# A recurrence and a gated feed-forward in one kernel: all steps put in a new order by a new table of due times

## The chip, the cores and the metric

The kernel runs on one core of a Trainium2 chip. The metric is the device time of one execution in microseconds (us). Before the change it is 270.87 us, the median of 13 runs that lie between 267.84 and 272.73 us.

## What is computed

The reference first runs a gated recurrence over 768 tokens for 4 batches and 8 heads of 48 columns each, and then a feed-forward layer with a sigmoid gate on its output:

```python
new_re = ar * S_re - ai * S_im
new_im = ar * S_im + ai * S_re
S_re, S_im = (new_re + kv, new_im)
y[:, :, t] = np.einsum('bhd,bhde->bhe', q[:, :, t], S_re)
...
gate = 1.0 / (1.0 + np.exp(-(x @ w_gate)))
val = x @ w_val
return (gate * val @ w_out).astype(np.float32)
```

Here `kv` is the outer product of a token's k and v, `ar` and `ai` are a decay of limited size, and x is y with the heads put side by side (3072 tokens of 384). The weights are 384 x 1536 (gate, value) and 1536 x 384 (out).

## The kernel before

**Tiles.** The work is cut into 24 slabs of 128 tokens: slab m is chunk m // 4 of batch m % 4. Slabs are taken together in groups of 2, 2, 4, 4, 4, 4, 2 and 2 (`SIZES`, L34). Group 0 is slabs 0 and 1, group 1 slabs 2 and 3, group 2 slabs 4 to 7, and so on; group 7 is slabs 22 and 23.

**Steps.** Each group's work is a list of small steps, each on one engine, with a name that the tables use. Per slab or group they are, in order of dependence:

- `lr`, `la`, `lk`, `lq`, `lv` (L560): loads of a_re, a_im, k, q and v on SP's queue, 192 KB each.
- `sq` (L587 on DVE for slabs 2 to 8, L590 on ACT for the others), `add` (L596), `min` (L603): squared size of the decay, limited; `add` and `min` are on POOL but for group 0.
- `lna`, `lnm`, `inv` (L611 to L622): logarithms and an inverse on ACT for a whole group; `r` (L628, POOL): a_im / a_re for two slabs at once; `atan` (L706, ACT): the angles of a group.
- `cl` (L637, PE): running sums of the logarithms; `ee` (L644, L646, ACT): their exponentials; `qke` (L699, POOL): q and k times these.
- `hop` (L718): a small accumulating DMA from POOL's queue that adds the angle of the chunk before; `ct` (L726, PE): running sums of angles; `r16`, `nid`: their whole turns taken off; `ab`, `cs`: sine and cosine on ACT; `ks`, `qs` (L784, DVE): k and q turned by them. In what follows they are called rotations.
- `tp` (L822, L823, PE) and `qkT` (L829, DVE): k and q transposed; from slab 13 on DMA transposes `xk`, `xq` (L805) on SP's queue do that. `sc` (L841, PE): scores; `mst` (L849, DVE): mask; `v16` (L692, POOL): v in 16 bits; `kv`, `P`, `u`, `x16`: the state carried from chunk to chunk; `y` (L907, L909, PE): result of the recurrence; `y16`, `xp`, `xt` (L526, L927, L933): scaled, transposed, put in place for the feed-forward.
- `pg`, `pv` (L946, PE): 12 blocks of 128 gate and value columns per group, three matmuls each; `tanh` (L956, ACT); `p` (L962, DVE): gate times value; `po` (L982, PE): product with the out weights, in thirds of four blocks; `ot` (L526, DVE) and `st` (L1000, SP): the output.
- `wg`, `wv`, `wo` (L545, L552): the weights, three pieces of 384 KB each, as DMAs from POOL's queue. Piece 0 of `wg` and `wv` serves blocks 0 to 3, piece 1 blocks 4 to 7, piece 2 blocks 8 to 11; piece i of `wo` serves `po` number i.

**What sets the order.** `TIMES` (L35) holds a due time for each step. `Plan.order` (L368) sorts all steps by it, and the steps are then issued in exactly this order, each into its own engine's queue; an engine works its queue off in that order and waits at a step whose inputs are not there. `SLOTS` tells which of the buffers of a kind each new tile takes, so that it fits the order. `WARM` tells how many matmuls of zeros by zeros (L1016) PE issues ahead of a step, into the place that this step then fills. A preload of an ACT function table (L1010) is put in wherever the order of ACT's steps asks for another table.

```python
order = sorted(self.steps, key=lambda k: (at[k], self.rank[k]))
...
for _ in range(WARM.get(key, 0)):
    nc.tensor.matmul(warm_of(tiles[st[2][0]]), zero, zero, start=True,
                     stop=True)
st[0](tiles)
```

PSUM has four banks for the recurrence (`gen`) and four for the feed-forward (`moe`).

Of the kernel before, what the change touches and what calls it, by code (L numbers as in the profile page):

```python
# [36 lines left out]
        26.449, 14.952, 43.624],  # L37
    "wv": [
        35.414, 39.921, 31.581],
    "wo": [  # L40
        54.9, 58.923, 61.61],
    "lr": [
        0.04, 0.86, 3.16, 7.96, 16.866, 21.689, 29.238, 27.449, 31.579,
        57.231, 51.953, 54.741, 61.401, 76.997, 73.157, 70.997, 97.193,
        107.417, 103.611, 112.215, 135.791, 138.231, 168.767, 169.177],
    "la": [
        0.45, 2.2, 6.04, 4.12, 20.729, 19.604, 26.489, 25.529, 32.539, 59.812,
        34.251, 50.545, 67.269, 76.037, 72.197, 71.407, 98.013, 102.041,
        108.375, 109.335, 147.165, 147.575, 169.587, 170.927],
    "sq": [  # L50
        3.77, 5.69, 9.53, 11.45, 24.478, 25.942, 36.28, 33.645, 42.515,
        67.879, 58.712, 64.157, 71.441, 83.336, 76.647, 75.036, 102.665,
        111.243, 113.196, 115.735, 154.358, 155.095, 174.405, 175.142],
    "add": [
        4.639, 6.559, 10.547, 12.518, 25.495, 32.621, 37.297, 38.966, 46.425,
        68.784, 59.963, 65.062, 72.346, 87.025, 78.508, 77.553, 103.57,
        112.148, 121.484, 118.991, 159.754, 161.154, 175.31, 176.265],
    "min": [
        7.139, 14.049, 33.685, 40.961, 70.553, 66.696, 88.09, 80.039, 115.263,
        125.354, 162.595, 177.329],  # L60
    "lna": [
        6.558, 12.482, 37.261, 79.205, 84.813, 120.672, 160.259, 179.013],
    "lnm": [
        8.163, 15.567, 41.927, 80.582, 92.638, 126.321, 163.562, 179.75],
    "inv": [
        7.426, 13.35, 38.769, 81.959, 94.015, 122.18, 161.127, 184.482],
    "r": [
        8.295, 15.772, 41.863, 44.664, 83.504, 85.265, 96.631, 116.166, 127.9,
        133.843, 163.498, 185.387],
    "cl": [  # L70
        9.051, 10.534, 24, 17.825, 49.018, 43.455, 50.689, 44.548, 82.679,
        89.335, 85.428, 88.289, 108.197, 107.551, 113.867, 103.467, 147.504,
        145.988, 149.897, 152.061, 178.984, 182.418, 181.772, 183.064],
    "ee": [
        14.827, 14.087, 24.847, 21.943, 50.8, 44.302, 51.54, 49.797, 84.073,
        91.158, 91.898, 90.418, 110.503, 109.763, 114.714, 111.98, 152.878,
        150.922, 152.138, 153.618, 180.487, 183.265, 191.04, 191.78],
    "scr": [
        15.383, 25.939, 41.172, 41.452, 56.111, 56.951, 56.391, 56.671,
        86.557, 95.304, 92.454, 90.974, 118.445, 111.665, 115.535, 114.545,  # L80
        155.82, 156.1, 157.07, 156.79, 193.097, 203.882, 196.626, 193.377],
    "rbe": [
        44.874, 64.632, 68.749, 99.353, 121.535, 159.55, 206.754, 198.964],
    "lk": [
        9.88, 7, 5.08, 23.609, 42.265, 40.762, 15.663, 22.649, 80.837, 78.917,
        79.877, 82.307, 114.135, 86.147, 110.295, 133.388, 111.255, 113.175,
        156.38, 140.993, 155.41, 165.821, 183.737, 176.887],
    "lq": [
        12.76, 10.84, 16.073, 24.569, 47.11, 49.021, 55.701, 38.864, 83.267,
        93.554, 84.227, 85.187, 117.045, 93.144, 118.035, 137.821, 123.663,  # L90
        115.125, 157.35, 142.018, 182.607, 175.347, 200.194, 177.847],
    "lv": [
        13.72, 8.92, 53.361, 36.65, 11.8, 74.117, 75.077, 77.957, 97.603,
        94.894, 107.007, 106.215, 119.025, 130.902, 92.734, 127.97, 178.878,
        102.451, 116.085, 126.118, 141.403, 174.387, 199.784, 218.157],
    "v16": [
        17.6, 13.473, 57.74, 54.324, 19.043, 79.462, 82.324, 82.9, 106.361,
        100.153, 109.945, 117.927, 129.876, 144.248, 104.703, 133.202,
        187.148, 127.324, 123.992, 178.232, 193.753, 219.214, 205.494, 221.697],
    "qke": [  # L100
        16.771, 14.973, 29.82, 28.059, 52.563, 55.72, 62.43, 50.728, 93.109,
        98.392, 94.87, 91.349, 135.604, 113.503, 137.365, 141.668, 153.8,
        151.844, 166.125, 156.048, 196.091, 189.765, 203.734, 194.33],
    "atan": [
        10.194, 19.172, 46.863, 87.484, 118.001, 148.251, 188.272, 189.009],
    "ct": [
        12.44, 11.347, 21.54, 25.148, 51.886, 53.61, 54.746, 56.6, 93.757,
        91.616, 94.403, 96.344, 130.858, 126.634, 134.942, 130.212, 155.052,
        165.217, 166.844, 166.03, 192.568, 198.999, 199.812, 200.458],
    "r16": [  # L110
        13.287, 12.367, 28.38, 27.914, 53.291, 54.61, 56.474, 63.368, 94.604,
        92.463, 97.821, 97.355, 134.447, 128.714, 135.789, 137.248, 156.004,
        166.559, 168.242, 167.31, 194.237, 202.477, 204.047, 205.555],
    "nid": [
        13.887, 13.086, 28.98, 28.514, 54.256, 56.047, 60.303, 64.307, 96.99,
        97.152, 100.067, 99.905, 136.883, 129.882, 138.988, 141.74, 157.444,
        167.49, 170.405, 169.595, 196.187, 205.189, 205.999, 208.104],
    "cr": [
        19.909, 20.279, 31.033, 29.876, 57.555, 59.712, 65.527, 64.894,
        101.555, 101.925, 107.622, 102.295, 140.822, 145.491, 142.418,  # L120
        145.861, 161.864, 174.035, 185.219, 176.848],
    "ab": [
        16.305, 15.839, 29.943, 28.878, 56.008, 56.94, 60.988, 66.098, 98.886],
    "cs": [
        18.385, 17.598, 30.246, 28.878, 56.504, 57.925, 63.37, 66.098, 99.749,
        98.115, 104.355, 105.988, 137.246, 130.246, 139.665, 142.788, 157.808,
        167.853, 170.768, 172.402, 196.551, 207.996, 206.363, 215.843],
    "ks": [
        21.351, 18.517, 35.11, 30.409, 57.423, 58.844, 64.766, 68.623,
        101.151, 102.017, 108.588, 107.277, 139.14, 131.535, 142.071, 146.825,  # L130
        159.333, 169.174, 173.51, 181.202, 200.279, 209.33, 208.464, 220.279],
    "qs": [
        22.217, 19.909, 37.146, 39.41, 61.787, 59.789, 67.757, 70.486,
        104.624, 102.883, 111.585, 109.454, 140.006, 132.401, 144.894,
        150.102, 163.262, 170.04, 180.336, 182.534, 201.611, 214.266, 211.395,
        221.145],
    "tp": [
        29.143, 23.217, 22.633, 22.186, 38.599, 38.146, 42.107, 44.101,
        67.888, 67.274, 60.789, 69.875, 80.555, 73.797, 79.709, 78.165,
        120.997, 111.232, 110.785, 112.326, 118.654, 113.42, 119.3, 117.557,  # L140
        154.605, 148.8],
    "qkT": [
        32.447, 23.879, 23.281, 25.344, 41.916, 41.318, 45.347, 44.749,
        72.304, 73.235, 64.167, 75.76, 84.348, 77.075, 80.758, 79.504,
        121.799, 116.734, 113.572, 112.974, 121.2, 116.136, 119.967, 118.205,
        155.405, 149.504],
    "sc": [
        33.18, 25.794, 28.183, 30.734, 51.335, 52.532, 49.943, 48.02, 77.191,
        77.415, 81.478, 78.612, 85.204, 86.52, 83.325, 86.297, 123.614,
        121.444, 114.513, 116.684, 122.317, 124.487, 125.76, 123.39, 156.571,  # L150
        157.607, 151.191, 147.281, 161.277, 156.348, 159.753, 157.83, 173.357,
        176.171, 186.3, 189.121, 193.214, 191.044, 196.35, 196.573, 214.294,
        216.66, 222.052, 221.178, 224.225, 225.498, 230.244, 231.777],
    "mst": [
        34.511, 27.315, 29.344, 33.046, 51.759, 55.076, 50.367, 52.691,
        78.438, 77.839, 82.488, 83.088, 85.629, 87.426, 83.749, 86.827,
        124.062, 122.397, 114.937, 117.333, 123.462, 125.593, 126.193,
        126.792, 157.535, 158.135, 151.615, 147.705, 161.731, 156.936,
        160.199, 158.734, 174.67, 179.137, 186.725, 189.545, 193.638, 191.469,
        196.774, 197.373, 216.613, 217.212, 223.542, 222.477, 224.892,  # L160
        225.957, 230.668, 232.202],
    "kv": [
        53.41, 33.403, 77.965, 71.96, 92.909, 105.408, 119.1, 119.747, 122.54,
        143.845, 153.357, 132.799, 171.215, 162.717, 164.617, 180.277,
        202.399, 215.812, 211.504, 228.006],
    "P": [
        53.811, 38.944, 79.038, 74.499, 95.07, 106.168, 119.501, 120.566,
        124.661, 146.359, 153.758, 133.267, 171.616, 165.096, 165.827,
        182.068, 207.399, 217.812, 213.8, 229.139],
    "y": [  # L170
        35.244, 37.788, 66.424, 58.18, 80.155, 84.525, 88.935, 87.889, 125.36,
# [875 lines left out]
```

## Time and profile before

| what | value |
|---|---|
| median of 13 runs | 270.87 us |
| lowest and highest run | 267.84, 272.73 us |
| the profiled execution: time | 268.61 us |
| its span, first to last instruction | 266.9 us |
| PE busy | 250.4 us (94%), of it 455 warming matmuls |
| DVE, ACT, POOL busy | 217.3, 182.8, 158.4 us |
| xt of slab 0 starts | 43.00 us |
| first gate matmul (block 5), first value matmul (block 0) of group 0 | 43.66, 47.63 us |
| hop of slab 4, ct of slab 4 start | 50.90, 54.72 us |
| first po of group 0 | 68.51 us |

How to read it: PE's busy row in the page has 40 slices of 6.7 us each, a 9 means full. Durations are those of the profiled execution. In a timeline, the numbers ahead of an engine are start and duration in us; in square brackets stands how long the engine was idle before the instruction, and what ended that. In a table by stretches, the two numbers behind the stretch's length are busy time and, in brackets, the number of instructions, for each engine.

### The profile page before, as it was taken

How to read it: one execution, taken by the hardware profiler on the slowest of the kernel's cores; microseconds unless marked ns; L12 is line 12 of the kernel's file. 1: busy time of each engine (PE TensorE's matmuls, PEld its weight loads, DVE VectorE, ACT ScalarE, POOL GpSimd, SP SyncE). 2: the span in 40 equal slices, each digit the busy share in tenths (PEclk: the TensorE clock that was granted, in tenths of full speed). 3: DMA queues.
4: the chain of work that ended last, by engine and by line, in shares of the span. 5: the costliest groups of instructions: out<-in, count | busy, mean ns of one | idle time of the engine just before them, and what ended most of it. 6: DMA issues, size and time to landing. Idle time of an engine off the chain costs nothing.

```text
span 266.9 us, 6422 instructions
## 1 busy us (share of the span) xinstructions
PE 250.4 (94%) x2435; PEld 171.8 (64%) x2435; DVE 217.3 (81%) x373; ACT 182.8 (68%) x304; POOL 158.4 (59%) x170
## 2 busy tenths in 40 slices
PE   8699979797889999999999999998999999999995
PEld 8477778665678764457764456754457645679784
DVE  3669999389999966999999988997765988988372
ACT  3987546966739999999666999768996375114340
POOL 1280769799369999549999379945479333201000
PEclk9899999999999999999999999999999999999999
DMA  7989999999999519999659897489962582951011
GB/s 149 227 141 201 200 220 186 163 186 162 125 191 216 110 36 190 144 203 200 98 132 201 173 167 132 81 173 147 225 130 43 118 113 41 196 129 52 0 61 59
DMA packets 175022, 38.18 MB, mean 143 GB/s; under 512 B 167928, under 2 KB 174992, under 8 KB 174992
## 3 DMA queue, kind: packets, MB, share of 16 engines
q1 hardware_dynamic: 170368, 34.20, 68.8%
q0 software_dynamic: 4624, 3.57, 9.2%
q8 instruction: 19, 0.31, 0.5%
q14 instruction: 11, 0.09, 0.1%
HBM read 30.74 MB, written 4.76 MB: 133 GB/s over the span
## 4 chain that ended last, share of the span: by engine, by line
PE 58%; DVE 13%; ACT 10%; DMA 6%; issue 5%; POOL 4%; SPq 3%; ACTq 0%; POOLq 0%; DVEq 0%
PE o L982 13%; PE v L946 13%; PE g L946 12%; DMA a<-in_a_im_dram 6%; PE ct L726 5%; PE cl L637 4%; PE sc L841 3%; DVE kst L784 3%; DVE mst L849 2%; SPq L560 2%; ACT g L956 2%; DVE qst L784 2%; POOL qk L699 2%; PE tp L822 1%; DVE y L526 1%
## 5 line engine op out<-in xcount | busy, mean ns | idle before, releaser
L956 ACT ACTIVATE g<-g 128x256 f16<-128x256 f32 (+1 forms) x96 | 45.7, 493 | 47.1 <-PE g L946 36.5
L962 DVE SCALAR_TENSOR_TENSOR p<-g,v 128x256 f16<-128x256 f16 (+1 forms) x96 | 50.9, 549 | 15.8 <-ACT g L956 11.4
L946 PE MATMUL v<-xt,wv 128*128 128x256 f16 (+1 forms) x288 | 58.7, 325 | 3.5 <-ACT g L956 2.7
L946 PE MATMUL g<-xt,wg 128*128 128x256 f16 (+1 forms) x288 | 57.8, 326 | 0.1
L982 PE MATMUL o<-wo,p 128*128 128x384 f16 (+1 forms) x300 | 55.8, 319 | 0.0
L699 POOL TENSOR_TENSOR qk<-qk,ee 128x768 f32<-128x768 f32 x22 | 43.0, 2104 | 8.0 <-DMA qk<-in_q_dram 5.4
L596 POOL TENSOR_TENSOR lm<-sq 128x384 f32<-128x384 f32 x22 | 24.2, 1103 | 32.5 <-DVE sq L587 19.7
L946 PEld LDWEIGHTS <-wv 128*128 128x128 f16 x288 | 26.6, 97 | 20.7 <-issue 6.0
L946 PEld LDWEIGHTS <-wg 128*128 128x128 f16 x288 | 27.4, 98 | 19.3 <-issue 2.6
L849 DVE TENSOR_TENSOR mst<-sc,msk_t 128x512 f16<-128x512 f32 x48 | 32.1, 685 | 9.2 <-PE sc L841 8.8
L982 PEld LDWEIGHTS <-p 128*128 128x128 f16 x300 | 27.0, 98 | 13.4 <-issue 0.9
L1010 ACT ACT_TABLE_LOAD x27 | 34.6, 1283 | 0.5
L1016 PEld LDWEIGHTS <-zero 128*128 128x128 f16 x455 | 29.1, 102 | 7.4 <-issue 3.9
L784 DVE TENSOR_TENSOR kst<-qk,cs 128x768 f16<-128x768 f32 x24 | 27.8, 1168 | 0.5 <-issue 0.2
L784 DVE TENSOR_TENSOR qst<-qk,cs 128x768 f16<-128x768 f32 x24 | 24.9, 1039 | 0.0
L637 PE MATMUL cl<-lm,wl_t 128*128 128x384 f32 x48 | 20.7, 523 | 3.1 <-ACT lm L617 2.6
L628 POOL TENSOR_TENSOR a<-a 128x768 f32<-128x768 f32 x11 | 21.5, 1958 | 1.7 <-ACT a L622 1.2
L863 POOL TENSOR_TENSOR state<-state,arr 128x384 f32<-128x384 f32 x16 | 14.4, 908 | 11.0 <-DVE state L891 10.5
L726 PE MATMUL ct<-a,wt_t 128*128 128x384 f32 x48 | 20.1, 511 | 0.3 <-ACT ee L644 0.2
L829 DVE COPY qkT<-tp 128x1024 f16<-128x1024 f16 x26 | 17.4, 685 | 1.7 <-PE tp L823 1.4
L718 POOL DMA_DIRECT2D a<-cr x20 | 16.9, 1073 | 2.5 <-ACT a L706 2.1
L692 POOL TENSOR_SCALAR v<-v 128x384 f16<-128x384 f32 x24 | 13.7, 569 | 7.7 <-DMA v<-in_v_dram 5.0
(72 smaller groups left out, 441.2 us busy)
## 6 DMA issues: line engine op xcount, KB each, us to landing
a<-in_a_re_dram SPq DMA_DIRECT2D x24, 192.0 KB
a<-in_a_im_dram SPq DMA_DIRECT2D x24, 192.0 KB
qk<-in_k_dram SPq DMA_DIRECT2D x24, 192.0 KB
v<-in_v_dram SPq DMA_DIRECT2D x24, 192.0 KB
qk<-in_q_dram SPq DMA_DIRECT2D x24, 192.0 KB
out_dram<-ot SPq DMA_DIRECT2D x23, 192.0 KB
wg<-in_moe_w_gate_dram POOLq DMA_DIRECT2D x3, 384.0 KB, 6.7
wv<-in_moe_w_val_dram POOLq DMA_DIRECT2D x3, 384.0 KB, 5.9
```

What stands on the lines that cost most here:

```text
L596: eng(g).tensor_tensor(out=T[LM][:, s], in0=T[SQ][:, 0], in1=T[SQ][:, 1], op=ALU.add)
L637: nc.tensor.matmul(T[CL][:, :HD], wl_t, T[LM][:, s], start=True, stop=True)
L699: eng(g).tensor_tensor(out=T[QK], in0=T[QK], in1=T[EE], op=ALU.mult)
L726: nc.tensor.matmul(T[CT][:, :HD], wt_t, T[A][:, 1, s], start=True, stop=False, skip_group_check=True)
L784: nc.vector.tensor_tensor(out=T[SL][i].rearrange("p h (r x) -> p h r x", r=2)[:, :, :, 0:D], in0=heads(T[QK][:, i]).unsqueeze(2) .broadcas ...
L849: nc.vector.tensor_tensor(out=T[MS], in0=T[SC], in1=msk_t.unsqueeze(1).broadcast_to([L, 4, L]), op=ALU.mult)
L946: nc.tensor.matmul(T[ACC][:, :nt], w[:, j, fb * 128:fb * 128 + 128], T[XT][:, j, :nt], start=(j == 0), stop=(j == 2))
L956: nc.scalar.activation(out=T[G16][:, :nt], in_=T[PG][:, :nt], func=FT.Tanh, scale=0.5)
L962: nc.vector.scalar_tensor_tensor(out=T[PT][:, fb, :nt], in0=T[G16][:, :nt], scalar=1.0, op0=ALU.add, in1=T[PV][:, :nt], op1=ALU.mult)
L982: nc.tensor.matmul(T[PO][:, :wd], T[PT][:, fb, s * L:(s + 1) * L], wo16[:, fb, c0:c0 + wd], start=(fb == 0), stop=(fb == NFB - 1))
L1010: nc.scalar.preload_act_table_set(SETS[key[1]])
L1016: nc.tensor.matmul(warm_of(tiles[st[2][0]]), zero, zero, start=True, stop=True)
```

## The change

No step, no tile and no instruction of the real work is changed; each stays on its engine. All numbers of `TIMES` are new, and with them the order of the steps on every engine, the buffers of `SLOTS`, and the places and numbers of the warming matmuls in `WARM` (455 before, 465 after). In the table a list's places are slabs (for `lr`, `la`, `sq`) or pieces (for the weights).

```diff
 TIMES = {
     "wg": [
-        26.449, 14.952, 43.624],
+        32.951, 14.583, 29.638],
     "wv": [
-        35.414, 39.921, 31.581],
+        41.185, 24.111, 37.481],
     "wo": [
-        54.9, 58.923, 61.61],
+        56.204, 51.226, 63.509],
     "lr": [
-        0.04, 0.86, 3.16, 7.96, 16.866, 21.689, 29.238, 27.449, 31.579,
-        57.231, 51.953, 54.741, 61.401, 76.997, 73.157, 70.997, 97.193,
-        107.417, 103.611, 112.215, 135.791, 138.231, 168.767, 169.177],
+        0.04, 0.86, 3.16, 5.08, 13.925, 19.752, 28.021, 17.531, 29.623,
+        62.128, 43.583, 64.048, 57.026, 74.047, 73.257, 65.008, 96.257,
+        107.615, 110.045, 101.515, 137.663, 151.768, 166.927, 171.067],
     "la": [
-        0.45, 2.2, 6.04, 4.12, 20.729, 19.604, 26.489, 25.529, 32.539, 59.812,
-        34.251, 50.545, 67.269, 76.037, 72.197, 71.407, 98.013, 102.041,
-        108.375, 109.335, 147.165, 147.575, 169.587, 170.927],
+        2.2, 0.45, 4.12, 7, 14.68, 15.64, 25.512, 24.552, 30.593, 69.119,
+        51.877, 58.495, 61.138, 75.967, 72.847, 63.088, 97.077, 105.695,
+        103.265, 102.675, 139.203, 141.828, 168.878, 168.468],
     "sq": [
-        3.77, 5.69, 9.53, 11.45, 24.478, 25.942, 36.28, 33.645, 42.515,
-        67.879, 58.712, 64.157, 71.441, 83.336, 76.647, 75.036, 102.665,
-        111.243, 113.196, 115.735, 154.358, 155.095, 174.405, 175.142],
+        5.69, 4.73, 9.161, 10.49, 21.424, 23.242, 34.706, 33.84, 44.15,
+        72.689, 57.636, 69.729, 66.044, 80.249, 76.577, 70.689, 104.472,
+        112.973, 118.73, 115.322, 149.228, 158.967, 174.676, 175.97],
...
 WARM = {
-    ('cl', 0): 87,
-    ('cl', 1): 15,
-    ('ct', 0): 8,
-    ('ct', 1): 3,
-    ('sc', 0, 0): 37,
-    ('y', 0): 12,
-    ('sc', 1, 0): 38,
-    ('sc', 1, 1): 12,
-    ('y', 1): 42,
-    ('pv', 0, 0): 5,
-    ('pg', 0, 3): 8,
-    ('pv', 0, 3): 3,
-    ('pv', 0, 4): 2,
-    ('pg', 0, 5): 24,
-    ('pv', 0, 7): 5,
-    ('pg', 0, 10): 6,
-    ('po', 0, 0): 3,
-    ('cl', 3): 51,
-    ('ct', 2): 55,
-    ('ct', 3): 9,
-    ('sc', 3, 0): 5,
-    ('sc', 3, 1): 8,
-    ('po', 2, 0): 4,
-    ('ct', 7): 7,
-    ('sc', 6, 0): 2,
-    ('sc', 7, 1): 4,
+    ('cl', 0): 86,
+    ('ct', 0): 19,
+    ('ct', 1): 18,
+    ('sc', 0, 0): 62,
+    ('sc', 0, 1): 4,
+    ('sc', 1, 0): 15,
+    ('sc', 1, 1): 18,
+    ('y', 1): 12,
+    ('pg', 0, 1): 3,
+    ('pg', 0, 3): 18,
+    ('pv', 0, 4): 13,
+    ('pg', 0, 7): 5,
+    ('pv', 0, 7): 8,
+    ('pg', 0, 10): 15,
+    ('cl', 2): 38,
+    ('cl', 3): 47,
+    ('ct', 2): 34,
+    ('ct', 3): 5,
+    ('y', 3): 12,
+    ('cl', 4): 6,
+    ('cl', 7): 23,
+    ('sc', 6, 0): 4,
 }
 SETOF = {"lna": "A", "lnm": "A", "inv": "AD", "ee": "AD", "atan": "BE",
          "tanh": "BCD", "cs": "CE"}
```

The weight pieces go out in the order wg1, wg0, wv2, wv0, wv1, wg2, wo0, wo1, wo2 before, and wg1, wv1, wg2, wg0, wv2, wv0, wo1, wo0, wo2 after. Group 0's blocks before begin with gates 5, 0, 4 and then value 0; after with value 0 and gates 6, 0, 3, values and gates then taking turns. The steps of POOL from the fifth sum on, and those of DVE around the rotations of slabs 4 to 7, stand in these orders (`k,b` is block b of group k, `m` a slab; for r and min the first of two slabs):

```
POOL before: add4 wg0 qke3 qke2 wv2 add5 min4 wv0 add6 add7 wv1 min6 r4 wg2 r6 add8 hop4-7 qke7 qke4
  v16 3 wo0 qke5 v16 2 wo1 add10 wo2 qke6 add11 min10 add9 min8 add12 arr2
POOL after:  add4 wv1 qke3 add5 qke2 wg2 min4 v16 0 wg0 add7 add6 wv2 min6 r6 wv0 r4 hop4-7 qke7 qke4
  wo1 qke5 add8 v16 3 wo0 v16 2 add10 qke6 wo2 add12 add11 min10 add15 add9 arr2
DVE before:  ks4 p0,7 ks5 qs5 p0,6 ab6 p0,4 qs4 p0,9 p0,1 r16 7 p0,10 qkT5 ks6 y16 3 ab7 p0,8 y16 2
  p0,11 qs6 ks7 xt2 xt3 ot1 qs7
DVE after:   ks4 r16 6 ks5 qs4 p0,2 p0,7 P0 ab6 p0,5 qs5 y16 3 qkT4 p0,4 p0,1 r16 7 qkT4 p0,10 ks6
  ab7 p0,11 y16 2 ks7 p0,9 p0,8 xt2 xt3 qs7 qs6
SP before, near group 7: lr22 lr23 la22 la23 xq17 xk17
SP after:                lr22 st9 st11 la23 la22 lk22 lr23 lk23 lv23 xq17 xk17
```

On DVE, four `qkT` copies, the square of slab 8 and three masks that stood behind group 0's xt now stand ahead of it. Group 2's last square is that of slab 6 in both; ahead of it two masks fewer (those of slab 1's second and slab 0's first half) and one rotation more (`qs` 2) stand than before.

## Prediction

> **What bounds the kernel now.** I read the page's busy rows first, then a table by stretches, then the timelines of the stretches in which PE is not full.
>
> ```profile
> PE   8699979797889999999999999998999999999995
> DVE  3669999389999966999999988997765988988372
> ```
>
> ```profile
> core 0: us, PE busy (x) PEld busy (x) DVE busy (x) ACT busy (x) POOL busy (x), PEclk, DMA share, GB/s
> ...
> 44.00:60.00 16.00, 14.23 (x132) 10.26 (x130) 10.36 (x19) 12.30 (x20) 14.27 (x13) 1.00 1.03 173
> 60.00:76.00 16.00, 12.75 (x131) 9.10 (x130) 15.72 (x25) 9.34 (x21) 11.46 (x10) 1.00 1.08 148
> 76.00:177.00 101.00, 100.11 (x944) 64.47 (x942) 91.29 (x156) 85.80 (x135) 83.10 (x87) 1.00 0.81 152
> 177.00:195.00 18.00, 16.66 (x94) 8.15 (x93) 13.36 (x20) 16.64 (x31) 7.20 (x8) 1.00 1.08 184
> ```
>
> From 76 us on PE is busy 100.11 of 101 us: its work sets the time there, and only two places interrupt it, both in the row 177:195 (16.66 of 18). Before 76 us PE waits or is fed with warming matmuls on zeros. From 60 to 76 us it is DVE that is full (15.72 of 16). So the end moves by three things: when PE's full stretch begins, what interrupts it, and how many warming matmuls are in it. The real work is the same before and after: 455 warming matmuls become 465, ACT's table loads stay 27, every other instruction has its partner.
>
> Why DVE is full is seen in its timeline, with POOL's and PE's beside it:
>
> ```profile
> 60.63 1.33 DVE L784 TENSOR_TENSOR kst<-qk,cs 128x768 f16<-128x768 f32 x1 [0.23 <-issue]
> ...
> 63.21 1.85 DVE L784 TENSOR_TENSOR qst<-qk,cs 128x768 f16<-128x768 f32 x1
> ...
> 66.11 1.52 DVE L784 TENSOR_TENSOR qst<-qk,cs 128x768 f16<-128x768 f32 x1
> ```
>
> ```profile
> 63.23 1.00 POOL L596 TENSOR_TENSOR lm<-sq 128x384 f32<-128x384 f32 x1
> 64.17 0.79 POOL L552 DMA_DIRECT2D wo<-in_moe_w_out_dram  x1
> 64.99 1.82 POOL L699 TENSOR_TENSOR qk<-qk,ee 128x768 f32<-128x768 f32 x1
> ```
>
> ```profile
> 65.12 0.23 PE L823 MATMUL tp<-idn_t,qst 128*128 128x128 f16 x1 [1.00 <-DVE qst L784]
> ...
> 68.02 0.49 PE L946 MATMUL v<-xt,wv 128*128 128x256 f16 x3 [0.65 <-DVE p L962]
> ```
>
> A rotation (ks, qs; L784) alone takes 0.95 us. The one at 63.21 takes 1.85: POOL's sum had just begun and ended at 64.23, and DVE ended 0.95 after some 64.1. The one at 66.11 ends 0.8 after POOL's product at 64.99. So a rotation that finds a POOL operation running waits for its end. In this stretch four are caught: 0.38 (60.63), 0.90, 0.57, and 0.80 at 73.48 (1.75 us), in all 2.65 us. Behind three of them PE is idle: 1.00, 0.65, and 0.74 at 75.56 behind xt: 2.39 us.
>
> The other interruption:
>
> ```profile
> 178.42 1.90 SPq L560 DMA_DIRECT2D a<-in_a_im_dram  x2
> 180.41 3.67 SPq L805 DMA_TRANSPOSE qkT<-qst  x1
> ```
>
> ```profile
> 185.09 0.84 ACT L590 ACTIVATE sq<-a 128x768 f32<-128x768 f32 x1 [1.11 <-DMA a<-in_a_im_dram]
> ```
>
> The square waits for the last load of group 7, a transpose is issued right behind that load, ACT's tanh queue stands behind the square, and PE idles 0.99 us before v at 186.60.
>
> **The change, part by part.** The due times of the table are used here only for which step stands ahead of which.
>
> *1. Group 2's rotation chain.* Its head is the last square (sq 6 on DVE, 38.62 us); then POOL's sums, two weight pieces, min and two products r, then atan, hop and ct. Behind the last square POOL has, before: two sums, wv1, min, r, wg2, r, and one sum of group 3; after: two sums, wv2, min, r, wv0, r. That is the same but for the sum, which hop 4 did not wait for (it waited 1.53 us for atan). So hop moves with the last square. DVE ran from 20 to 40 us at 19.4 of 20. Ahead of the last square the new order has two masks less (mst, 0.68 each) and one rotation more (0.95): -0.4. Port waits ahead of it were sq5 +0.5, ks3 +0.9 (1.84 us, behind POOL's qk product of slab 2), sq7 +0.6: 2.0. In the new order ks2 comes first and needs the later product itself, so neither rotation can run into qk; what can be in the way is min (0.83) and v16 (0.51). I take 0.9 for 2.0: -1.1. The load of sq 6 is 27th instead of 29th on SP and was landed at 35 us, so it binds neither way. The chain comes 1.5 us sooner; DVE idles 5.6 us between 44 and 60, waiting mostly for it, but group 0's xt now stands behind three masks, four copies and a square that it led before. Bounds 0 and -1.5; I take the middle, **-0.7**.
>
> *2. Value weights.* All nine pieces cost POOL as before (0.79 to 0.85 each). New is that wv0, which the first value matmul reads, is the last piece, and that PE's queue has ct 4 behind that matmul. From issue at t it lands at t+5.7 to t+6.4 (the three wv), 6.7 at worst (wg). From v to ct 4 PE has four pieces of 0.33, scores 0.22 and 18 warming ones of 0.055 (six took 0.33, from 62.34 to 62.67): 2.5 us, so ct 4 could go at t+8.2 to t+9.2. But ct 4 needs the r behind wv0: in the trace 8.13 us pass from r's start to ct 4 (46.60 to 54.72), so t+0.85+8.13 = t+9.0. The wait lies in the shadow of hop's chain: 0 to +0.3, **+0.1**. Without that cover it would be up to 1.0.
>
> *3. Port waits between ks4 and qs7.* POOL's operations that read SBUF there are, before: qk 1.84, v 0.5, sum 1.0, qk 1.82, sum 1.0, min 0.83, sum 1.0, min 0.83 = 8.8 us. After: sum 1.0, v 0.5, v 0.5, sum 1.0, qk 1.82, sum 1.0 = 5.8, since one qk and the two mins moved out. 2.65 x 5.8/8.8 = 1.75, so 0.9 less on DVE, and PE's gaps follow nearly one to one. Bounds: -2.4 (none caught) and +1 (qk of slab 6, which now stands right beside qs5, taken whole instead of in part: 1.8 for 0.9). **-0.9**.
>
> Here the rule weighs. The Trainium skill (SBUF — State Buffer, Who interferes with whom) says that a DVE instruction with two SBUF inputs and a GpSimd one that reads SBUF lock each other out for the whole instruction, by issue order; that writing descriptors doesn't count is marked there as inferred. The row decides: at 63.21 the wo descriptors (64.17, 0.79) follow the sum without a pause, and DVE ends at 65.06, which is 0.95 behind the sum and not behind the descriptors. Were they part of the lock, moving wo1 and wo2 would be worth up to 1.6 us more; by the row it is worth nothing.
>
> *4. Group 7's loads.* On SP the last of them (lr 23) is now followed by a k and a v load before the first transpose. A load takes 2.2 to 2.9 us alone and took 5.5 with the transpose beside it. The square comes in time: **-1.0**, bounds 0 (another load late) and -1.1.
>
> *5. Warming matmuls.* Ten more at 0.055 = +0.5 if on the path; nearly all stand before 62 us, where PE waits anyway: **+0.1**.
>
> *6. 76 to 255 us.* The order is new everywhere, PE is full, so nothing can be gained but the one place of step 4 and gaps of 0.45 and 0.35 us (110 and 193 us), while each new wait costs in full. Bounds 0 and +2; **+0.5**, about the size of those two small gaps.
>
> Sum: -0.7 +0.1 -0.9 -1.0 +0.1 +0.5 = -1.9 us. The profiled execution took 268.61 us (span 266.9 and 1.7 around it): 266.7. The median of the 13 runs lies 2.26 above it, within their 267.84 to 272.73; with the same difference, **269.0**.
>
> **Rivals.** *B, the waits only move.* POOL takes the port before qs5, ks6 and ks7 as often as before, and the earlier chain is eaten by group 0's late xt: steps 1 and 3 give 0, the sum is -0.3, the time 270.6. For it: a port wait hangs on some tenths of a us. Against it: 3 us less of POOL work in the stretch.
>
> *C, slower: DVE's slack from 120 to 160 us is used up.* DVE is busy 38.3 of 40 us there with PE at 39.8. Today's port waits (ks13 0.7, ks14 1.2, ks12 0.2, qs and ks16 some 0.5: 2.6) are just covered; PE shows no gap. The new order puts POOL's r, qk14 and qk15 (1.8 each) beside ks12, qs12 and ks14. Three caught whole are 5.4, 2.8 more, against 1.7 of idle DVE, which products p and PSUM banks use already. At one to one on PE, with B elsewhere: +2.5, 273.4. It decides from 1.7 us of added port wait in that stretch (-0.3 + 1.7 = +1.4). Against it: the same number of rotations and POOL operations stands there as before.
>
> **How the numbers follow.** A 0.48, B 0.22, C 0.30; C is high because a new order has a hundred places to lose and PE is full for 180 us. A's own range: -5.0 (all lower bounds) to about 0, 265.9 to 270.9. With B and C 8 in 10 lie in 265.8 to 273.4. This kernel's measurement tells about 0.5% (1.35 us) from no change. A lies beyond it in 0.42 of its 0.48, else within; B gives 0.05 faster, 0.16 same, 0.01 slower; C 0.02 same, 0.28 slower: faster 0.47, same 0.24, slower 0.29.
>
> **What would show it.** Step 1: sq 6 near 37 us, hop 4 near 49.4. Step 2: the first v matmul waits for a DMA, ct 4 no later than 9 us after wv0. Step 3: L784 sums to less than 52.7 us (27.8 and 24.9 now), PE gaps from 57 to 75 us under 1.5. Step 4: no wait of a square for a DMA near 180 us, none on PE. C: L784 over 1.8 us after 120 and PE idle there. I am wrong if PE is full later than 76 us, or if its gaps after it sum to over 3 us.

## The result and the profile after

The changed kernel takes 265.48 us, the median of 11 runs from 264.82 to 267.71. The kernel before took 270.93 beside it, the median of 48 runs from 267.84 to 273.52. The medians differ by 5.45 us; the ratio is 0.985, with an interval of 0.9814 to 0.9885. (The ratio leaves out the runs that lie over 1.5% above a kernel's fastest, 12 of the 48, and so shows 4.0 us of the 5.45.) I had forecast 269.0, a gain of 1.9. The direction is right and the size isn't.

The profiled execution took 266.53 us, with a span of 264.7: 2.08 less than the profiled execution of before. By that one pair of profiles the forecast of -1.9 would look exact.

The page's busy rows and granted clock (line numbers after are 4 lower than before, since the tables are shorter):

```profile
PE   8598897799899999999999999999999999999995
DVE  2659899369999964999989988988668978986552
PEclk9889999999999999999999999999999999999999
```

The table by stretches, the columns as in the prediction:

```profile
44.00:60.00 16.00, 14.00 (x130) 9.92 (x127) 9.34 (x18) 11.50 (x22) 14.06 (x13) 1.00 0.88 143
60.00:76.00 16.00, 15.07 (x192) 12.61 (x191) 15.55 (x28) 8.47 (x21) 6.84 (x7) 1.00 1.05 173
76.00:177.00 101.00, 100.72 (x934) 64.59 (x932) 90.17 (x155) 87.82 (x138) 87.48 (x90) 1.00 0.83 153
177.00:195.00 18.00, 17.82 (x103) 8.76 (x100) 14.14 (x22) 17.56 (x31) 9.72 (x12) 1.00 1.03 204
```

PE is busy 2.32 us longer between 60 and 76 us (15.07 for 12.75), 1.16 between 177 and 195, and 0.61 between; from 44 to 60 it is 0.23 less. Most of the 2.32 is work on zeros: 51 warming matmuls (3.66 us) run between 60 and 76 where 16 (1.54 us) did. The first gate block of group 1 starts at 75.04 us, where it stood at 76.00. Of the page's groups, the two rotations:

```profile
L780 DVE TENSOR_TENSOR kst<-qk,cs 128x768 f16<-128x768 f32 x24 | 25.3, 1053 | 2.5 <-ACT cs L770 1.6 <-issue 0.7
L780 DVE TENSOR_TENSOR qst<-qk,cs 128x768 f16<-128x768 f32 x24 | 24.8, 1035 | 0.0
```

They sum to 50.1 us (52.7 before). Three timelines of after, of DVE, POOL and PE:

```profile
65.25 2.06 DVE L780 TENSOR_TENSOR qst<-qk,cs 128x768 f16<-128x768 f32 x1
```

```profile
64.67 1.82 POOL L695 TENSOR_TENSOR qk<-qk,ee 128x768 f32<-128x768 f32 x1 [0.72 <-DMA qk<-in_q_dram]
66.43 0.82 POOL L548 DMA_DIRECT2D wo<-in_moe_w_out_dram  x1
```

```profile
51.65 0.50 PE L942 MATMUL v<-xt,wv 128*128 128x256 f16 x3 [0.83 <-DMA wv<-in_moe_w_val_dram]
```

One rotation of the stretch waits long: qs 5 starts 0.58 us into POOL's product, takes 2.06 us and ends 0.82 after the product (66.49). It is the only one over 1.75, and PE loses 0.88 us behind it. The third fence is new: the first value matmul waits 0.83 us for its weights, which were issued at 44.73 and landed 6.9 us later.

### The profile page after: what moved, and what is told of

It reads as the page before. It is cut to its first block, busy times and chain, and to the rows that moved or that the text cites. A ratio compares the mean times of both kernels' runs of the same rounds, so it can differ in the third digit from the quotient of the medians.

```text
span 264.7 us, 6444 instructions
## 1 busy us (share of the span) xinstructions
PE 250.8 (95%) x2445; PEld 173.4 (66%) x2445; DVE 211.5 (80%) x373; ACT 182.4 (69%) x304; POOL 160.9 (61%) x170
## 4 chain that ended last, share of the span: by engine, by line
PE 62%; ACT 9%; DVE 9%; DMA 9%; SPq 5%; issue 3%; POOL 2%; DVEq 0%; ACTq 0%
PE v L942 15%; PE o L978 15%; PE g L942 14%; SPq L556 5%; PE cl L633 4%; PE ct L722 3%; PE sc L837 3%; DMA qk<-in_k_dram 3%; DMA wv<-in_moe_w_val_dram 3%; DMA a<-in_a_re_dram 2%; DVE qkT L825 2%; ACT L1006 1%; DMA a<-in_a_im_dram 1%; PE y L905 1%; ACT g L952 1%
## 5 line engine op out<-in xcount | busy, mean ns | idle before, releaser
L952 ACT ACTIVATE g<-g 128x256 f16<-128x256 f32 (+1 forms) x96 | 44.6, 491 | 37.9 <-PE g L942 29.4
L592 POOL TENSOR_TENSOR lm<-sq 128x384 f32<-128x384 f32 x22 | 27.9, 1269 | 32.7 <-DVE sq L583 17.2
L942 PEld LDWEIGHTS <-wv 128*128 128x128 f16 x288 | 27.3, 98 | 21.7 <-issue 3.4
L1012 PEld LDWEIGHTS <-zero 128*128 128x128 f16 x465 | 30.1, 104 | 6.9 <-issue 5.3
L780 DVE TENSOR_TENSOR kst<-qk,cs 128x768 f16<-128x768 f32 x24 | 25.3, 1053 | 2.5 <-ACT cs L770 1.6
L633 PE MATMUL cl<-lm,wl_t 128*128 128x384 f32 x48 | 19.8, 512 | 3.4 <-ACT lm L613 2.7
L624 POOL TENSOR_TENSOR a<-a 128x768 f32<-128x768 f32 x11 | 19.9, 1812 | 3.4 <-ACT a L618 3.2
L728 DVE TENSOR_SCALAR r<-ct 128x384 f16<-128x384 f32 x24 | 13.1, 551 | 7.7 <-PE ct L722 7.6
L768 ACT ACTIVATE cs<-ct 128x384 f32<-128x384 f32 x24 | 11.8, 491 | 10.6 <-DVE cs L756 10.6
L688 POOL TENSOR_SCALAR v<-v 128x384 f16<-128x384 f32 x24 | 15.4, 642 | 5.1 <-DMA v<-in_v_dram 3.1
```

What stands on the lines that cost most here:

```text
L592: eng(g).tensor_tensor(out=T[LM][:, s], in0=T[SQ][:, 0], in1=T[SQ][:, 1], op=ALU.add)
L633: nc.tensor.matmul(T[CL][:, :HD], wl_t, T[LM][:, s], start=True, stop=True)
L780: nc.vector.tensor_tensor(out=T[SL][i].rearrange("p h (r x) -> p h r x", r=2)[:, :, :, 0:D], in0=heads(T[QK][:, i]).unsqueeze(2) .broadcas ...
L942: nc.tensor.matmul(T[ACC][:, :nt], w[:, j, fb * 128:fb * 128 + 128], T[XT][:, j, :nt], start=(j == 0), stop=(j == 2))
L952: nc.scalar.activation(out=T[G16][:, :nt], in_=T[PG][:, :nt], func=FT.Tanh, scale=0.5)
```

## The experiments

Each edit changes due times of `TIMES` or a number of `WARM` and nothing else. Runs are named b_ when they start from the kernel before and a_ when they start from the changed one.

### The kernel before, unchanged

> The kernel before, unchanged, for its spread. Its 48 runs lie between 267.8 and 273.5 us, those after the change between 264.8 and 267.7; the two profiled executions differ by only 2.1 us, the medians by 5.4. Theory M (many small waits): the old order has waits that hang on tenths of a us, and in its long runs, of 271 to 273 us, PE's idle time after 44 us is 2 to 4 us larger than the 7 us or so of the profiled one of 268.6, in more than one place. Theory K (clock): the long runs are those whose TensorE clock was granted late at the start; then their mean clock is lower by 0.005 or more and PE's gaps after 44 us are the same. Theory L (loads): the long runs have one long wait for a load, 2 us or more.

The 12 runs have a median of 270.61 us and fall into two groups: 267.90 to 268.36 (five runs, mean granted clock 0.999 or more) and 270.56 to 272.20 (seven, clock 0.987 to 0.994). The 48 runs of the kernel before quoted above do the same: 19 lie between 267.84 and 269.11, 29 between 270.02 and 273.52, none in between. The profile fell on a short run, like the one that I predicted from. Its timelines of DVE, PE and ACT at the three places of the prediction:

```profile
63.89 1.75 DVE L784 TENSOR_TENSOR qst<-qk,cs 128x768 f16<-128x768 f32 x1
```

```profile
65.70 0.23 PE L823 MATMUL tp<-idn_t,qst 128*128 128x128 f16 x1 [0.90 <-DVE qst L784]
```

```profile
183.98 1.83 ACT L590 ACTIVATE sq<-a 128x768 f32<-128x768 f32 x2
```

The port wait is there as before (1.75, and 0.90 on PE). The wait of the last square is not: the two squares run without a pause. Nor do four of the runs below that keep the old order there (b_add10, b_flip, b_qs5b, b_warm) show PE idle over 0.36 us between 180 and 196. So the 0.99 us that step 4 wanted to save is lost in one profiled execution of six.

### The transpose behind group 7's loads, alone

```diff
 }
+TIMES["xq"][4] = 177.0; TIMES["xk"][4] = 177.2   # before
```

> The kernel before, with only the two transposes of slab 17 moved on SP behind the next four loads. Step 4 of the prediction: the last load of group 7 then lands 2.3 to 3.0 us after its issue, the square near 184 us no longer waits for it, and the time falls by 1.0 us against the kernel before. Rival: the wait was hidden by the order behind it, PE idles at the next step instead, and the time falls by less than 0.4.

Measured: 270.90 us, ratio 1.0089 (1.0043 to 1.0134): no gain. It is longer, since 10 of the 12 runs are of the longer group, where 9 of the 23 beside it are; why more of them are isn't known, since the edit moves nothing ahead of 160 us. All 12 have a clock of 0.994 or less. The square's wait is gone, but the profile fell on a long run and shows what such a run is. DVE, POOL and PE around the rotation qs 5:

```profile
63.81 4.50 DVE L784 TENSOR_TENSOR qst<-qk,cs 128x768 f16<-128x768 f32 x1
```

```profile
63.07 0.82 POOL L552 DMA_DIRECT2D wo<-in_moe_w_out_dram  x1
63.92 1.01 POOL L596 TENSOR_TENSOR lm<-sq 128x384 f32<-128x384 f32 x1
64.86 0.79 POOL L552 DMA_DIRECT2D wo<-in_moe_w_out_dram  x1
65.67 1.81 POOL L699 TENSOR_TENSOR qk<-qk,ee 128x768 f32<-128x768 f32 x1
```

```profile
68.37 0.29 PE L823 MATMUL tp<-idn_t,qst 128*128 128x128 f16 x1 [3.65 <-DVE qst L784]
68.45 0.31 PE L822 MATMUL tp<-idn_t,kst 128*128 128x128 f16 x1
68.56 0.31 PE L823 MATMUL tp<-idn_t,qst 128*128 128x128 f16 x1
```

```profile
60.00:76.00 16.00, 11.39 (x99) 8.03 (x97) 14.53 (x21) 8.68 (x20) 9.51 (x8) 0.89 1.15 160
```

The same rotation that took 1.75 or 1.85 us now takes 4.50. It starts 0.11 us ahead of POOL's sum, is passed by it, doesn't get in while the descriptors of wo are written (64.86 to 65.65), is passed by the product too, and ends 0.83 us after it. PE, which needs it, idles 3.65 us. Behind that, matmuls start 0.11 us apart (68.45, 68.56) instead of 0.055: the granted clock is 0.5 from 68.33 to 71.74 us, which the stretch shows as a mean of 0.89. The first gate block of group 1 starts at 80.1 us, 3.5 later than in the short run. That is more than the 2.7 us by which the spans of this run and of the short one differ: from that block to the end it takes 189.2 us, against 189.4 to 190.0 in the five profiles without the square's wait, so the edit saves at most some tenths. Up to 160 us this is the kernel before.

### The weights in another order on the changed kernel

```diff
 }
+TIMES["wg"][0] = 24.111; TIMES["wv"][0] = 29.638; TIMES["wv"][2] = 32.951   # after
+TIMES["wv"][1] = 37.481; TIMES["wg"][2] = 41.185
```

> The kernel after, with only the weight pieces dealt to POOL's places in another order: wg1, wg0, wv0, wv2, wv1, wg2 in place of wg1, wv1, wg2, wg0, wv2, wv0. The first value matmul then finds its weights and its wait of 0.83 us near 51 us is gone. Step 2 of the prediction (the wait lies in the shadow of hop's chain): 0 to -0.3 us against the kernel after. Rival (the wait is on PE's path, everything behind it moves): -0.8, about 264.7 median.

Measured: 264.93 us (after: 265.48 and, measured again, 265.29). The profiled execution has the same clock as that of after (0.992), so the two can be laid side by side:

```profile
49.19 1.56 PE L633 MATMUL cl<-lm,wl_t 128*128 128x384 f32 x4 [0.71 <-DVE xt L929]
50.59 0.49 PE L942 MATMUL v<-xt,wv 128*128 128x256 f16 x3
```

The 0.83 us in front of the first value block is gone. ct 4 starts at 53.12 instead of 54.20, and group 1's first gate block at 74.43 instead of 75.04. So the late wv 0 costs some 0.6 us in such an execution, and 0.4 between the medians, which is about as much as runs scatter. The cover of step 2 was not whole.

### One sum of group 3 ahead of the hops

```diff
 }
+TIMES["add"][8] = 45.3   # after
```

> The kernel after, with only POOL's sum of slab 8 moved ahead of group 2's hops, where the order before had it. If hop's chain sets when DVE's full stretch begins (step 1), the hops and all behind them come up to 1.0 us later and the time rises by 0.5 to 1.0 against the kernel after. Rival: hop 4 waits for atan anyway while the sum runs, and ct 4 waits for the value matmul; nothing changes (within 0.2).

Measured: 264.88 us. hop 4 starts at 48.75 us in the profiled execution, ct 4 at 52.20; in the changed kernel with a whole clock (a_again, below) they stand at 48.01 and 52.26. So the first 0.7 us of delay at the hop cost nothing, as the rival had it: the sum that stood in front of the hops in the kernel before does no harm there, and its removal isn't the source of the gain.

### What passes the rotation: two edits of the kernel before

```diff
 }
+TIMES["add"][10] = 62.44   # before: sum of slab 10 behind wo 2 and qke 6
```

> The kernel before, with only POOL's sum of slab 10 moved behind wo2 and the product qk of slab 6, so that it no longer stands right beside the rotation qs of slab 5. Theory M2 (the spread of the kernel before is one rotation that is passed by two POOL operations in a row: 4.50 us and 3.65 us of idle PE in the profile of a long run, 1.75 to 1.85 us and 0.90 to 1.00 in short ones): the wait is gone or is one operation long, no run is above 269.5, the median 267.5 to 268.3. Theory K (a late TensorE clock alone makes the long runs): half of the runs stay at 270.5 to 272.5.

```diff
 }
+TIMES["wo"][2] = 62.44   # before: wo 2 behind qke 6
```

> The kernel before, with only wo2 moved behind the product qk of slab 6, so that sum and product follow each other on POOL without the weights' descriptors between them. Theory M2: qs of slab 5 loses to both every time, L784 of slab 5 takes 3.5 us or more in the profile, and the runs gather at 270 to 272 also with a full clock. Rival: the rotation gets in at the sum's end, as in the short runs; times as the kernel before in its short runs, 268.2, and one more wait on POOL.

The first gives 270.29 us, the kernel before beside it 268.56 (13 of its 22 runs are short ones here); the ratio is 1.0079 (1.0044 to 1.0114). Only one run (268.83) is at the shorter group's level, so the expectation that the long runs would go fell: the wait only moved. The second gives 268.95 us, 267.43 to 270.64, with a ratio of 1.0012 (0.9967 to 1.0057): its longest runs are shorter, and no gain is shown. Of its expectations, the rotation lost to both operations, but the runs did not gather at 270 to 272. The rotations that were passed in the two profiles, and PE behind the first:

```profile
62.94 3.92 DVE L784 TENSOR_TENSOR kst<-qk,cs 128x768 f16<-128x768 f32 x1 [0.42 <-POOL v L692]
```

```profile
66.91 0.29 PE L822 MATMUL tp<-idn_t,kst 128*128 128x128 f16 x1 [2.24 <-DVE kst L784]
```

```profile
62.79 3.74 DVE L784 TENSOR_TENSOR qst<-qk,cs 128x768 f16<-128x768 f32 x1
```

In the first, ks 5 takes the place of qs 5. It is held through two writings of descriptors (62.62 to 64.20) and the product, and the half clock lasts 6.83 us. In the second, with the descriptors of wo 2 moved behind the product, the rotation is still passed, but 0.76 us sooner free (3.74 for 4.50), which is the time of one writing of descriptors (0.79). PE's gap there is 3.06 us and the half clock lasts 3.41.

### The same rotation later

```diff
 }
+TIMES["qs"][5] = 62.3   # after: behind y16 3 and two p
```

> The kernel after, with only the rotation qs of slab 5 moved on DVE behind y16 3, one copy qkT and two products p. In the profile after it stood behind qk of slab 6 and took 2.06 us, and PE was idle 0.88 us before a value matmul that waits for a product p. If that port wait is what is left of step 3: qs takes 0.95 to 1.2, the PE gap is below 0.3, and the time falls by 0.6 to 0.9, to about 264.7. Rival: DVE is full there anyway or the rotation is late for the transposes of slab 5; within 0.3 of the kernel after.

```diff
 }
+TIMES["p"][4] = 60.68; TIMES["qs"][5] = 60.7; TIMES["tp"][10] = 61.62   # before
```

> The kernel before, with the rotation qs of slab 5 put behind the products p of blocks 6 and 4 (it starts some 2 us later, by which time POOL's sum of slab 10 and its product for slab 6 are over or nearly so), and with the PE transposes that need it behind two more feed-forward blocks. Theory P (the rotation that two POOL operations in a row pass, PE's idle time of 3 us behind it and the half clock that follows are what separates the kernel before's longer runs from its shorter ones): no rotation over 2.9 us between 57 and 70 us, no half clock after 44 us, no run above 269.5, median 267.0 to 268.2. Theory K (the half clock comes by itself, the idle time is only where it shows): about half of the runs stay at 270 or more. Should another rotation be passed in its place, as in the run that moved the sum of slab 10, this tells nothing of P or K.

On the changed kernel: 265.51 us, no gain. The wait of qs 5 and PE's 0.88 us are gone, but gaps of 0.36 and 0.68 us appear at the ct of slabs 11 and 13. On the kernel before: 270.91 us, all 12 runs at 270.26 or above, with a clock of 0.987 to 0.994. qs 5 now starts 0.66 us later than in the long run above, within the descriptors of wo 2, and is passed by the product alone:

```profile
64.47 3.27 DVE L784 TENSOR_TENSOR qst<-qk,cs 128x768 f16<-128x768 f32 x1
```

PE idles 2.83 us, and the clock is 0.5 for 3.41 us again. The edit missed its aim and, as said beforehand for this case, tells nothing of the two theories. As its runs look, a place 0.7 us away can turn a wait that is met in some of them into one that is met in all.

### Warming matmuls in the place of PE's idle time

```diff
 WARM = {
-    ('pv', 0, 4): 2,
+    ('pv', 0, 4): 60,
```

> The kernel before, with 60 warming matmuls in place of 2 ahead of value block 4 of group 0, the place at which PE idles for the passed rotation; 58 x 0.055 = 3.2 us of PE work on zeros that lie in the idle time when the rotation is passed and are lost when it isn't. Theory P (the half clock follows from PE's idle time): no half clock after 60 us, whether qs of slab 5 is passed or not; runs that were near 268.2 rise by some 2.2 (3.2 less the idle 1.0) to 270.4, runs that were near 271 stay or fall by the half clock's share, so all gather at 269.5 to 270.8 and none is above 271.3. Theory K (the half clock comes by itself): granted clock of 0.5 for 3.4 us or more behind the passed rotation in some runs still, with times up to 273.

Measured: 269.13 us, where the kernel before beside it has 271.28; all 12 runs lie between 268.52 and 270.11, and those of before between 267.55 and 273.0. The ratio, which leaves out the longest runs of before, is 0.9983 (0.9947 to 1.0019): the shorter runs gain nothing, the longer ones are gone. The page's clock row, DVE, and PE:

```profile
PEclk9999999999999999999999999999999999999999
```

```profile
63.00 4.57 DVE L784 TENSOR_TENSOR qst<-qk,cs 128x768 f16<-128x768 f32 x1
```

```profile
62.92 3.51 PE L1016 MATMUL v<-zero 128*128 128x128 f16 x60
...
67.62 0.23 PE L823 MATMUL tp<-idn_t,qst 128*128 128x128 f16 x1 [0.64 <-DVE qst L784]
```

The rotation is passed exactly as in the long run (4.57 us), but PE is fed meanwhile and idles 0.64 us, and the clock stays whole. So the half clock follows from PE's idle time, not the other way round. The runs gather about 1 us lower than I had expected.

### The changed kernel again, and the chain of hops

> The kernel after, unchanged, for a profile with a full clock; its first profile has half clock from 11.3 to 14.8 us. Both theories: a run with a full clock is 264.8 to 265.5; its group 1 starts its first gate block at 73.5 to 74.0 us, against 76.6 in the profile of the kernel before with a full clock, and from there to the end it takes 189.5 to 190 us, as the kernel before. That would put the whole gain of full-clock runs, 3 us, before that block.

Measured: 265.29 us; the profile fell on an execution with the whole clock from start to end, as that of b_again did. That pair shows where the shorter runs gain. POOL and PE:

```profile
48.01 1.68 POOL L714 DMA_DIRECT2D a<-cr  x2 [1.82 <-ACT a L702]
```

```profile
52.26 1.13 PE L722 MATMUL ct<-a,wt_t 128*128 128x384 f32 x3
```

| starts at, us | before again | after again | difference |
|---|---|---|---|
| sq 6 | 39.03 | 37.28 | -1.75 |
| hop 4 | 51.32 | 48.01 | -3.31 |
| ct 4 | 55.40 | 52.26 | -3.14 |
| ks 4 | 61.31 | 57.40 | -3.91 |
| first gate block of group 1 | 76.61 | 73.29 | -3.32 |
| from there to the span's end | 190.0 | 189.9 | -0.1 |

The whole gain lies ahead of 76 us. To test whether hop's chain carries it, I held the hops back behind POOL's product for slab 7. The kernel is the best one below, and only the hops and ct 4 differ:

```diff
 }
+TIMES["hop"][0] = 49.45; TIMES["hop"][1] = 49.451; TIMES["hop"][2] = 49.452   # a_best
+TIMES["hop"][3] = 49.453; TIMES["ct"][4] = 49.46
```

> The same three edits, and POOL's four hops of group 2 moved behind the product qk of slab 7, which takes 1.8 us. If the chain of group 2's rotations sets when PE's full stretch begins (step 1), ct 4, ks 4 and the first gate block of group 1 come 1.2 to 1.8 us later and the time rises by as much, to 265.8 or more. If DVE's order behind it has slack, less than 0.4.

Measured: 267.20 us, against 264.62 without. POOL and PE:

```profile
51.53 2.46 POOL L714 DMA_DIRECT2D a<-cr  x3
```

```profile
54.64 0.88 PE L722 MATMUL ct<-a,wt_t 128*128 128x384 f32 x2 [2.72 <-DMA a<-cr]
```

hop 4 comes 2.8 us later (the product ahead of it had to wait for its factors, so the delay is larger than expected), PE idles 2.72 us, ct 4 and group 1's first gate block (75.08 for 72.47) come 2.6 later, and so does the end. Nothing behind ct 4 takes any of it up, so a hop this late costs in full. It doesn't show that the 3.3 us gained came by this chain alone: in a_again PE goes from a gate block to ct 4 without idling, so that there its own queue sets ct 4, and in a_add8 a hop 0.7 us later moved nothing. Two of the 12 runs, 269.52 and 269.87 us, show a clock of 0.987 and 0.986; no trace shows where they lost it.

### The best version, and one more use of warming

a_best puts the three edits of the changed kernel together (weights, add 8, qs 5); a_warm0 adds 40 warming matmuls at the start:

```diff
 WARM = {
-    ('cl', 0): 86,
+    ('cl', 0): 126,
```

> The kernel after with three edits together: the weight pieces dealt wg1, wg0, wv0, wv2, wv1, wg2, the sum of slab 8 ahead of group 2's hops, and qs of slab 5 behind two products. The first two gave 264.9 each against 265.5. If PE gaps before 76 us add up one to one: 263.8 to 264.2. Rival: they share one slack, and the time stays at 264.9.

> The kernel after with the three edits of the best version so far (weight pieces, sum of slab 8, qs of slab 5), and 126 in place of 86 warming matmuls ahead of the first sums cl 0, where PE idles 2.7 us before them. Theory W (this idle time lets the clock drop at 11 us in a third of the runs, and that costs 1.0): all runs have a mean clock of 0.996 or more and lie at 264.2 to 264.8. Rival: the drop depends on what PE does after cl 0; it stays in some runs.

a_best: 264.62 us, 264.26 to 265.59, ratio to before 0.9867 (0.9829 to 0.9906). It is 0.7 below the changed kernel in medians (265.29), between its expectation and the rival's; the ratios to before (0.9867, and 0.9883 and 0.985 for the changed kernel) don't tell them apart. a_warm0: 264.76 us. The half clock that some executions have between 11 and 15 us (the two 8s of the first clock row above) is in none of its six runs by their mean clock (0.998 or more), where a third of the changed kernel's runs seem to have it; but one run has 266.97, with a gap of 1.62 us at 238 us. No gain is left over.

## Why the prediction was right in direction and wrong in size

**From the profile to the median: the step that failed.** The prediction says: "The median of the 13 runs lies 2.26 above it, within their 267.84 to 272.73; with the same difference, 269.0". I took the 2.26 for something that both kernels have. It is a property of the kernel before: its median falls among the 29 longer runs of 48, in which, as far as the profiles show, qs 5 is passed by two POOL operations, PE idles about 3 us, and the clock is halved behind that. The 19 shorter runs have a median of 268.61, so of the 5.45 us the change gains 3.13 against the shorter runs, and 2.32 because it has no longer ones. (No long run of the unedited kernel was profiled. That they are of this kind rests on the run with an edit far behind, on the clock, which is 0.981 to 0.994 in 46 of the 49 longer runs of this kernel for which it is on record, and on the warming matmuls, which take them all away.) The profile showed a run in which qs 5 was passed once. The changed kernel has POOL's product ahead of wo 2 there, qs 5 takes 1.88 to 2.20 in four profiles, PE idles about 1 us, and the long runs don't occur; its median lies 1.05 below its profiled execution (265.48 and 266.53), because that execution had a half clock at the start. With the profile's own 266.7 as the forecast I would have been 1.2 off instead of 3.5. A spread of 267.84 to 272.73 in a kernel on one core was a question to ask, not a constant to carry over.

**Step 1, group 2's rotation chain: right in sign, undersized.** Foretold -0.7 (bounds 0 and -1.5). In the pair with the whole clock hop 4 moved by -3.31, in the first pair by -1.67 (50.90 to 49.23). Held back by 2.8 us, it costs 2.6. Group 1's first gate block moved by -3.32 in the pair with the whole clock, where steps 1, 2, 3 and 5 together had -1.4; how much of that comes by the hops and how much by PE's own new order wasn't separated. The failing sentence is "hop moves with the last square". From the last square's start to hop 4 pass 12.28 us before and 10.75 after. Two things make the 1.5. Behind the last square's end POOL needs 2.70 us for the two sums before and 1.82 after (39.56 to 42.26; 39.43 to 41.25), since the sum of slab 7 now runs beside that square. And ACT no longer has group 0's first two tanh ahead of atan:

```profile
48.58 0.66 ACT L956 ACTIVATE g<-g 128x256 f16<-128x256 f32 x2
49.12 1.49 ACT L706 ACTIVATE a<-a 128x1536 f32<-128x1536 f32 x1
```

```profile
47.44 1.48 ACT L702 ACTIVATE a<-a 128x1536 f32<-128x1536 f32 x1 [1.74 <-POOL a L624]
```

The first fence is the trace of before: r ended at 48.42, and atan started at 49.12 behind them. The second is after: ACT waits, and atan starts 0.03 us after r. I had compared POOL's order on this chain and not ACT's. What remains, -1.75 at sq 6 in one pair and -0.14 in the other, was foretold as -1.1. The pairs differ by the half clock near the start, which both executions of the pair with -0.14 have (from 10.71 us before, from 11.34 after). The changed kernel's order pays for it and the old one doesn't: sq 6 starts at 38.48 and 38.52 us in its two profiles with that half clock, and at 37.08 to 37.56 in its six without; in the old order at 38.57 and 38.62 with it, and at 38.34 to 39.29 without.

**Step 2, value weights: the sign right, the cover partly absent.** Foretold +0.1. The wait was there in one profiled execution (0.83 us on PE; landing in 6.9 us, where I had 6.7 as the worst), and not in the other. The edit that takes it away gains 0.4 to 0.6, which is not clear of the scatter.

**Step 3, port waits: right in size in the short runs.** Foretold 2.65 to 1.75 us. After, ks 4, qs 4 and qs 5 lose 0.15, 0.33 and 1.11, in all 1.6. PE's gaps from 57 to 75 us are 0.88, under the 1.5 that I named. The bound with "qk of slab 6" came in part: qs 5 waited through the last 1.24 us of that product and lost 1.11, more than the 0.90 before; the gain is in ks 4, qs 4 and ks 7 (0.38, 0.57 and 0.80 before). But the row that I let decide about descriptors decides for its own run only. There DVE came in at the sum's end, while the descriptors of wo were written; in the long runs it stood through them, and moving them behind the product freed it 0.76 us sooner. So "worth nothing" was wrong: they cost nothing in one run and 0.8 us of the rotation's wait in another. The Trainium skill (SBUF — State Buffer, Who interferes with whom) has the lock go by issue order. The long run speaks against that: the rotation starts at 63.81, ahead of the sum (63.92) and of the product (65.67), and runs behind both. (Times on POOL are rough, so the 0.11 us to the sum prove little; the 1.86 to the product do.) What makes the difference isn't settled. In the five profiles with a wait over 3 us the rotation began while descriptors were being written; in the two short ones of the kernel before, qs 5 began with the sum or just behind it. But ks 5 of b_again began within descriptors too (63.02) and took 0.96.

**Step 4, group 7's loads: fell.** Foretold -1.0. The wait is gone after, as I said. But it isn't in b_again either, whose end from group 1's first gate block on takes the same 190 us as that of after, and the edit alone gained nothing that shows. I had read a wait of one execution, one of six profiled, as a cost of every one.

**Step 5 and step 6.** What the ten warming matmuls more cost, no run shows. Nearly all of the 465 do stand before 62 us, but the surplus doesn't: in the first pair 419 start ahead of 62 us where 434 did, and 46 behind it where 21 did. From group 1's first gate block on: -0.1 instead of +0.5. Rival C did not come: after 120 us no rotation takes over 1.8 us and PE is full. Rival B fell with the sum over L784 and PE's gaps. That the sum of -1.9 came out as -2.08 in the first pair of profiles is luck: ahead of group 1's first gate block that pair has -0.96 where -1.4 was foretold, since the half clock at the start held the changed kernel up, and behind it -1.2 for -0.5, since the execution before had the wait of step 4. In the pair with the whole clock the sum is -3.4.

## What to carry to other kernels

Where a kernel's runs fall into two groups, find what a long run looks like before you forecast: a change that takes the long runs away gains more than any sum over the profile of a short one shows. A short wait of PE and a long one differ by more than their lengths, since the clock is lost behind the long one; work on zeros in its place costs less (269.13 us, where the longer runs beside it have a median of 271.58 and the shorter ones of 268.40). When a chain is followed from engine to engine, compare the order on each engine that it passes through, and not only on the one with most steps of it.

## What the runs showed of the hardware

- A rotation on DVE (two SBUF inputs, 0.95 us alone) was passed by two successive POOL operations and by the descriptors between them: 4.50 and 4.57 us. I had expected one at most.
- PE gaps of 2.24 with 1.38, 2.83, 3.06 and 3.65 us were each followed by a clock of 0.5 for 3.41 or 6.83 us; gaps of 0.64 to 1.62 us were not, nor were one of 2.72 us that ended at 54.64 us and seven of 1.91 to 2.18 us near 10 us. The Trainium skill (TensorE: Matmul & The Clock Gate, Part 1: The HAM clock gate) has the clock fall after an idle window of some 3.4 us; the 3.41 agrees with the length of the stretches here, but gaps shorter than it were enough.
- What tells these gaps apart is how they lie in time. In every trace the stretches between two changes of the clock are whole multiples of 3.41 us (3.41, 6.83, 61.44, 197.97, 259.41). When windows of that length are laid out from a change of the clock, PE's idle time in one window goes with the clock of the next, as in these rows:

| run | window, us | PE idle in it, us | clock of the next window |
|---|---|---|---|
| b_xq_late | 64.91 to 68.33 | 3.42 | 0.5 |
| b_flip | 63.87 to 67.28 | 2.72 | 0.5 |
| before | 7.30 to 10.71 | 2.38 | 0.5 |
| b_add10 | 63.05 to 66.46 | 2.31 | 0.5 |
| b_qs5b | 65.53 to 68.94 | 2.26 | 0.5 |
| a_warm0 | 236.59 to 240.00 | 1.62 | 1.0 |
| a_hoplate | 49.92 to 53.34 | 1.42 | 1.0 |
| a_hoplate | 53.34 to 56.75 | 1.30 | 1.0 |

By this reading the gap of 2.72 us in a_hoplate did no harm because the end of a window split it. In the 13 traces with a change of the clock, every window with 2.26 us or more of idle PE was followed by a half clock, and none with 1.62 or less was; in b_add10 one with 1.83, itself at half clock, was followed by a second. No run was made to move a gap against the windows.

- A half clock of 3.41 us between 10.7 and 14.8 us came in some executions of either kernel and not in others. It goes with PE's gap ahead of the first sums `cl` 0: 2.38 to 2.85 us in the four profiles with it, 0.51 to 2.18 in the eleven without. In the changed kernel the runs with a mean clock under 0.995, which this half clock would explain, are about 1 us longer (medians of 265.2 and 266.2 us in 11 and 7 executions).
